# Zeros for the output: two transfers from SyncE's queue, or twelve from ScalarE's

## The chip, the cores and the metric

One Trainium2 chip; the kernel runs on one of its cores. The metric is device microseconds of the whole program, lower is better. Engines: TensorE (PE, with its weight loads as PEld), VectorE (DVE), ScalarE (ACT), GpSimd (POOL) and SyncE (SP). SP and ACT issue plain DMAs, POOL the indirect ones (gathers and scatters by a list of rows).

## The reference

A linear attention whose output feeds a mixture of 8 experts, of which each of 3072 tokens uses two:

```python
# attention: q, k, v [4, 8, 768, 64], in blocks of 64 with a decaying state
intra = (qb @ kb.T * Dmask) @ vb
inter = (qb * lam_pow) @ kv_state
x = attn_out.transpose(0, 2, 1, 3).reshape(3072, 512)
# mixture
noisy = x @ w_gate + log1p(exp(x @ w_noise)) * noise      # [3072, 8]
top2 = argpartition(-noisy, 2)[:, :2]; w = softmax of the two
out = zeros((3072, 512))
for e in range(8):
    for k in range(2):
        mask = top2[:, k] == e
        h = maximum(x[mask] @ w1[e], 0)                   # w1[e] 512 x 1024
        out[mask] += w[mask, k] * (h @ w2[e])             # w2[e] 1024 x 512
```

Everything is float32. A token that is not expert 0's gets its first contribution by an addition into `out`, so `out` has to hold zeros before the experts write to it.

## The kernel before, in words

The program has three stretches.

**Attention** goes in 12 steps (`for t in range(NST)`), two chunks of 128 tokens each. Each step stores its rows to a DRAM tensor `x_tok` (`store_x`, L443) and computes gate logits.

**Routing** is done in three groups of chunks, 0 to 7, 8 to 15 and 16 to 23. For each chunk and each of its two choices POOL scatters 128 records (token number and weight, 8 bytes each) to the lists `lst` in DRAM: 48 scatters (`scatter_list`, L634), handed out one to three at a time by `paced`, which first copies one element of a tile that the scatter is to come after (`spacer`, L682). The lists of the other experts are read back with `load_rec` (L880, L882): `recz` for expert 0, `rec` for the rest. The first `rec` load needs all 48 scatters; the second `recz` load needs those of the first two groups, 32 scatters. They stand on SP's queue, which is worked through in order.

**Experts**: expert 0 is computed in three parts of 2, 2 and 3 tiles of 128 tokens (`PARTS0`, the last tile 64). In each part eight blocks of the first layer (`mm1`, 12 matmuls each, L1037, into one of four PSUM banks `pS`) are evacuated by ACT (`ht`, L1043) and DVE (L1047), then `gemm2` (24 matmuls a tile, L1078, or 16 for the last) follows. In the third part, between the `gemm2` of its tiles, PE transposes the rows that POOL has gathered for expert 1 (`trans_rows`, L898, from `gather_rows`, L889). PE works in program order, so it stands there until the gather has landed. The weights of expert 1 (`w1`, six loads, L770) are loaded from SP's queue after the second part. The experts' outputs are scattered into `out` from expert 1's first layer on (`scatter_out`, L1135).

The zeros for `out` come from one 128 x 512 tile `zero`, read again and again: 24 blocks of 128 rows, 6 MB in all. The tile is later also the output tile of expert 0's last `gemm2` (`PV`, L1089).

The order is that of the program. For DMAs of SP and ACT together the framework hands out eight semaphores in turn (DMAHW0 to DMAHW7), in the order in which it expects the DMAs to be issued; a DMA is issued when the one that had its semaphore before has landed. POOL's DMAs have eight others (DMASW0 to DMASW7).

Of the kernel before, what the change touches and what calls it, by code (L numbers as in the profile page):

```python
# [35 lines left out]
DM = H * D  # L36
# [4 lines left out]
NTOK = B * S  # L41
# [25 lines left out]
LOADS = {2: [(1, 0)], 3: [(1, 1)], 4: [(1, 2)], 5: [(1, 3)], 9: [(2, 0), (2, 1)], 10: [(2, 2)], 11: [(2, 3)]}  # L67
HIGH = {4: [(1, 0)], 5: [(1, 1)], 6: [(1, 2)], 7: [(1, 3)], 10: [(2, 0), (2, 1)]}
LOW = {5: [(1, 0)], 6: [(1, 1)], 7: [(1, 2)], 10: [(2, 0)]}
ZEROS = {11: 8}  # L70
LATE = (6, 7)
MID = 16
X1 = ((), (), (), (), (0, 1), (2, 3, 4), (5, 6))
# [17 lines left out]
def size(e, t):  # L91
    return TS if t < NT - 1 else TAILS[e]
# [31 lines left out]
def kernel(  # L124
# [3 lines left out]
    nc = tc.nc  # L128
# [22 lines left out]
    def load(u, nm):  # L151

        if u >= NST:
            return
        b, w = divmod(u, NW)
        at = b * H * S * D + w * 2 * C * D
        store, src, n = {"qt": (QT, q, 2), "kt": (KT, k, 2), "vt": (VT, v, 3)}[nm]
        store[u] = aw.tile([128, 2, H, D], FT, name=nm, bufs=n)
        for a in range(2):
            nc.sync.dma_start(store[u][:, a], sub(src, at + a * C * D, [[D, 128], [S * D, H], [1, D]]))  # L160
# [36 lines left out]
    p = psum.tile([128, H], FT, name="pL")  # L197
# [13 lines left out]
    p = psum.tile([128, HP, C], FT, name="pL")  # L211
# [88 lines left out]
    def scatter(n):  # L300
        for job in scatters[:n]:
            scatter_list(*job)
        del scatters[:n]
# [11 lines left out]
    def trans_k(u):  # L315

        kT[u] = aw.tile([128, HP, 2, C], FT, name="kT", bufs=1)
        for a in range(2):
            p = bank()
            for hp in range(HP):  # L320
                nc.tensor.transpose(p[:, hp, :], KT[u][:, a, 2 * hp:2 * hp + 2, :], identf)
            if u:
                nc.scalar.activation(kT[u][:, :, a, :], p, AF.Copy)
            else:
                nc.vector.tensor_copy(kT[u][:, :, a, :], p)
# [62 lines left out]
    def intra(u):  # L388
        for hp in range(HP):
            for a in range(2):  # L390
                for s in range(2):
                    add_out(u, a, hp, s, VT[u][:, a, 2 * hp + s, :], AT[u][hp // 2][:, s, hp % 2, a, :])
# [28 lines left out]
    def products(u):  # L421

        p = psum.tile([128, 2, C], FT, name="pR")
        for d in range(DB):
            nc.tensor.matmul(p[d * 32:(d + 1) * 32], wgn[:, d, :], XO[u][:, :, d, :], start=True, stop=True)
        XP[u] = aw.tile([128, 2, C], FT, name="xp", bufs=1)
        nc.scalar.activation(XP[u], p, AF.Copy)
# [3 lines left out]
    def turn_x(u):  # L431

        XC[u] = aw.tile([128, 2, DB, C], FT, name="xc")
        for a in range(2):
            p = bank()
            for d in range(DB):
                nc.tensor.transpose(p[:, d, :], XO[u][:, a, d, :], identf)  # L437
            nc.scalar.activation(XC[u][:, a], p, AF.Copy)

    def store_x(u):  # L440

        queue = nc.gpsimd if u < NST - 4 else nc.sync
        queue.dma_start(x_tok[2 * u * C:2 * (u + 1) * C, :].rearrange("(a p) m -> p a m", a=2),  # L443
                          XC[u].rearrange("p a d i -> p a (d i)"))
# [235 lines left out]
    def paced(n, tile):  # L680
        if scatters:
            nc.gpsimd.tensor_copy(spacer, tile[0:1, 0:1])  # L682
            scatter(n)
# [9 lines left out]
    for n in range(2):  # L693
        o, m = n * DB * CAP, DB * TX * TS
# [149 lines left out]
    def split_low(which, e, j, half=None, low=nc.vector):  # L844
        for st, hi, lo in split_parts(which, e, j, half):
            low.tensor_tensor(lo, st, hi.bitcast(FT), op=SUB)
# [182 lines left out]
    def columns(e, t0, n):  # L1029
        return slice(t0 * TS, min((t0 + n) * TS, FULL + TAILS[e]))  # L1030
# [19 lines left out]
    def ht(e, part, f, c):  # L1050

        at = c.start + (0 if not part else TAILS[e] if c.start >= FULL else CAP + TAIL)
        return HT[0].rearrange("p (f c) -> p f c", f=FB)[:, f, at:at + c.stop - c.start]
# [90 lines left out]
    zero = consts.tile([128, DM], FT, name="zero")  # L1144
# [4 lines left out]
    def zero_out(n):  # L1149
        i = list(itertools.islice(zeros, n))  # L1150
        if i:
            nc.sync.dma_start(out[i[0] * 128:(i[-1] + 1) * 128, :].rearrange("(a p) m -> p a m", p=128),
                              zero[:, None, :].to_broadcast([128, len(i), DM]))

    for t in range(NST):
        u = t + 1
        if t:
            products(t - 1)
            turn_x(t - 1)
            if t == 8:  # L1160
                split_low(1, 0, 3, low=nc.gpsimd)
        if u < NST:
            trans_k(u)
        load(t + 3, "kt")
        if u < NST:
            trans_q(u)
        load(t + 3, "qt")
        if u < NST:
            kv(u)
        if t:  # L1170
            store_x(t - 1)
            paced(1, XC[t - 1][:, 1, 0, :])
        if t not in LATE:
            kdecay(t + 2)
        if u == NST:
            scatter(1)
        if u == NST:
            logits(t - 1)
        intra(t)
        load(t + 3, "vt")  # L1180
        inter(t, 0)
        evac_o(t)
        if t in LATE:
            kdecay(t + 2)
        paced(1, XO[t][:, 1, 0, :])
        if t and u < NST:
            logits(t - 1)
        if 2 * t in GB[1:]:
            if 2 * t > GB[1]:
                finish(GB.index(2 * t) - 2, False)  # L1190
            jobs.append(routing(GB.index(2 * t) - 1))
        advance(FILLB)
        if u < NST:
            scores(u)
            inter(u, 1)
        for which, j in HIGH.get(t, []):
            split_high(which, 0, j)
        if u < NST:
            if LOW.get(t):
                nc.gpsimd.tensor_copy(spacer, AT[u][0][0:1, 0, 0, 0, 0:1])  # L1200
            for which, j in LOW.get(t, []):
                split_low(which, 0, j, low=nc.gpsimd)
            paced(1, AT[u][1][:, 1, 0, 0, :])
        advance(FILLA.get(t, 18))
        for which, j in LOADS.get(t, []):
            load_w(which, 0, j)
        zero_out(ZEROS.get(t, 0))
        if t == 2:
            turn_noise()
        if t == 4:  # L1210
            for i in range(4):
                nc.sync.dma_start(sub(lst, i * 128 * LI * RW, [[LI * RW, 128], [1, LI * RW]]), linit)
# [30 lines left out]
    for i, (t0, n) in enumerate(parts(0)):  # L1243
        for f in range(FB):
            if i or f >= 2:
                gemm1(0, t0, n, f)
            if i == 0:
                if 1 <= f < 5:
                    split_w(2, 0, 2 + (f > 2), (f - 1) % 2)
                if f == 2:  # L1250
                    nc.scalar.activation(XG[6], zero, AF.Copy)
                advance(FILL1)
            if i == 1 and f < 4:
                advance(FILL2)
                if f == 3:
                    finish(2, False)
            if i or f >= 2:
                paced(1 + (i == 2), ht(0, 0, f, columns(0, t0, n)).bitcast(FT))
            if i == 1 and f == 2:
                load_rec(0, 1)  # L1260
            if i == 2 and f == 2:
                load_rec(1, 0)
                load_rec(0, 2)
                load_rec(0, 3)
                for j in range(1, 3):
                    load_rec(1, j)
                for t in range(NT):
                    gather_rows(1, t)
            if i == 2 and f >= 4:
                for j in X1[f - 4]:  # L1270
                    trans_rows(j, size(1, j))
        if i == 0:
            zero_out(NTOK // 128)
            advance(50)
        if i == 1:
            which_expert(1, nc.sync)
            which_list(1, nc.sync)
            for j in range(4):
                load_w(1, 1, j)
        for t in range(t0, t0 + n):  # L1280
            if i < 2:
                paced(3, PV[t - 1] if t > t0 else ht(0, 0, FB - 1, columns(0, t0, n)).bitcast(FT))
            for _ in gemm2(0, t):
                pass
            if t == 0:
                advance(50)
            for j in {0: (2, 3), 2: (4, 5, 6)}.get(t, ()):
                trans_rows(j, size(0, j))
            if i == 2:
                for j in range((0, 2, 4)[t - t0], (2, 4, 4)[t - t0]):  # L1290
                    split_w(1, 1, j)
                    load_w(2, 1, j)
                for j in X1[t]:
                    trans_rows(j, size(1, j))
# [225 lines left out]
    with tc.For_i(0, n_over) as it:  # L1520
# [16 lines left out]
        for f in range(FB):  # L1537
            p = psum.tile([128, OV], FT, name="pS", bufs=4)
# [7 lines left out]
        p = psum.tile([OV, DM], FT, name="pO")  # L1546
# [35 lines left out]
```

## Time and profile before

| | us |
|---|---|
| median of 3 runs | 692.43 (691.93 to 693.0) |
| the profiled execution | 693.23 |
| its span, from the first to the last instruction | 691.4 |
| PE busy in the span | 671.6 (97%) |
| granted TensorE clock, mean | 0.994 |

How to read it: times in the rows below are microseconds from the span's start. The first two columns of a row of the timeline are its start and its length; what stands in square brackets is how long the engine sat idle before it and what ended that. An SPq or ACTq row is the issue of a DMA by that engine's sequencer; the transfer itself comes after it. "To landing" is from the issue to the arrival of the DMA's semaphore. In the tables of windows the columns give each engine's busy time, and at the end the granted clock, the busy share of the 16 DMA engines and the rate.

### The profile page before, as it was taken

Reading aid. Unit: us, or ns where it says so; the run is one execution under the profiler, and the core shown is the slowest. Engines: PE = TensorE matmul, PEld = TensorE weight load, DVE = VectorE, ACT = ScalarE, POOL = GpSimd, SP = SyncE. Lnnn points to the kernel's source line nnn. Section 1 sums busy time; section 2 is a strip of 40 time slices with the busy share of each in tenths; the row PEclk is TensorE's granted clock in tenths of the full one; section 3 lists DMA queues with packets and bytes.
Section 4 is the critical chain, followed back from the end, with each engine's and each line's share of the span. In section 5 each row is a group of like instructions: output and inputs, shape, how many; then the busy total and the mean of one; then the engine's idle time right before and its main releaser. Section 6 shows DMA issues by size and latency. Waiting matters only on the chain.

```text
span 691.4 us, 13961 instructions
## 1 busy us (share of the span) xinstructions
PE 671.6 (97%) x4861; PEld 598.1 (87%) x4861; DVE 482.4 (70%) x1060; ACT 309.5 (45%) x634; POOL 370.0 (54%) x474
## 2 busy tenths in 40 slices
PE   7899999899999999999999999999999999999995
PEld 4788888698898898899989998998898899889984
DVE  6335888878436566789867886889596979588610
ACT  2667786441133332365437434653363356327400
POOL 7111355678854555776358536753773667264332
PEclk9999999999999999999999999999999999999998
DMA  9999999576517437766477547854875576464033
GB/s 205 214 233 262 229 252 250 163 245 163 113 32 221 136 119 171 175 177 191 149 183 188 189 149 178 221 175 142 166 235 158 126 195 189 122 135 116 1 46 40
DMA packets 151901, 115.06 MB, mean 166 GB/s; under 512 B 88063, under 2 KB 123007, under 8 KB 151828
## 3 DMA queue, kind: packets, MB, share of 16 engines
q1 hardware_dynamic: 137636, 84.04, 44.8%
q0 software_dynamic: 13776, 29.57, 20.5%
q8 instruction: 39, 0.64, 0.4%
q10 hardware_dynamic: 416, 0.53, 0.3%
q14 instruction: 34, 0.28, 0.1%
HBM read 77.58 MB, written 37.32 MB: 166 GB/s over the span
## 4 chain that ended last, share of the span: by engine, by line
PE 68%; DVE 12%; issue 8%; POOL 4%; DMA 3%; SPq 2%; ACT 1%; POOLq 1%; DVEq 0%
PE pS L993 15%; PE pKV L1078 13%; PE pO L1078 10%; PE pS L1037 7%; PE pS L1110 5%; PE pS L364 3%; PE pKV L377 2%; POOL lst L634 2%; PE pO L377 2%; SPq L160 2%; PE pR L993 1%; POOL out_dram L1135 1%; DMA xr<-x_tok,rec 1%; DVE ht L1004 1%; PE pS L437 1%
## 5 line engine op out<-in xcount | busy, mean ns | idle before, releaser
L993 PE MATMUL pS<-xa,w 128*128 128x400 f32 (+1 forms) x624 | 158.0, 343 | 0.3 <-ACT gt L1012 0.2
L818 POOL TENSOR_TENSOR wst<-wst 128x256 f32<-128x256 f32 x96 | 96.4, 1016 | 84.1 <-DVE w L810 81.7
L993 PEld LDWEIGHTS pS<-xa,w 128*128 128x128 f32 x624 | 113.2, 188 | 4.6 <-DVE w L810 2.0
L1135 POOL DMA_INDIRECT out_dram<-ot,rec x40 | 73.6, 1839 | 75.5 <-DVE ot L1094 56.2
L1078 PE MATMUL pKV<-w2h,ht 128*128 128x512 f32 x336 | 109.0, 394 | 0.0
L1078 PE MATMUL pO<-w2h,ht 128*128 128x512 f32 x336 | 108.4, 392 | 0.0
L993 PE MATMUL pS<-xb,w 128*128 128x400 f32 (+1 forms) x240 | 81.6, 340 | 0.0
L1078 PEld LDWEIGHTS pKV<-w2h,ht 128*128 128x128 f32 x336 | 63.2, 188 | 14.3 <-DVE gt L1094 0.6
L1078 PEld LDWEIGHTS pO<-w2h,ht 128*128 128x128 f32 x336 | 63.1, 188 | 13.5
L1037 PE MATMUL pS<-xa,w 128*128 128x256 f32 (+2 forms) x440 | 73.5, 316 | 0.8 <-DVE xa L901 0.4
L1037 PEld LDWEIGHTS pS<-xa,w 128*128 128x128 f32 x440 | 65.3, 189 | 4.9 <-DVE xa L901 0.6
L1078 PE MATMUL pKV<-w2l,ht 128*128 128x512 f32 x168 | 65.8, 391 | 0.0
L1078 PE MATMUL pO<-w2l,ht 128*128 128x512 f32 x168 | 65.7, 391 | 0.0
L961 ACT ACTIVATE xa<-wst 128x512 fp32r<-128x512 f32 (+1 forms) x48 | 25.1, 568 | 79.5 <-DVE wst L970 72.3
L810 DVE TENSOR_TENSOR w<-wst,w 128x512 fp32r<-128x512 f32 (+2 forms) x72 | 59.6, 844 | 0.1
L889 POOL DMA_INDIRECT xr<-x_tok,rec x42 | 46.2, 1101 | 19.2 <-issue 6.5
L634 POOL DMA_INDIRECT lst<-recs,dest x48 | 49.7, 1035 | 10.8 <-issue 8.5
L1012 ACT ACTIVATE ot<-pS 128x400 f32<-128x400 f32 (+1 forms) x60 | 29.7, 495 | 48.8 <-PE pS L993 44.6
L808 ACT ACTIVATE w<-wst 128x512 fp32r<-128x512 f32 (+2 forms) x72 | 48.1, 692 | 5.3 <-POOL wst L818 5.2
L1004 DVE SCALAR_TENSOR_TENSOR ht<-ot,ht 128x400 fp32r<-128x400 f32 (+1 forms) x60 | 45.4, 756 | 1.5 <-ACT ht L1001 0.8
L993 PEld LDWEIGHTS pS<-xb,w 128*128 128x128 f32 x240 | 45.0, 188 | 0.6 <-DVE xb L962 0.3
L1043 ACT ACTIVATE ht<-pS 128x256 fp32r<-128x256 f32 (+2 forms) x40 | 17.9, 448 | 59.5 <-PE pS L1037 58.2
(287 smaller groups left out, 1367.0 us busy)
## 6 DMA issues: line engine op xcount, KB each, us to landing
wst<-in_moe_w_dram SPq DMA_DIRECT2D x36, 512.0 KB, 5.4
wst<-in_moe_w_dram SPq DMA_DIRECT2D x32, 256.0 KB, 3.3
kt<-in_k_dram SPq DMA_DIRECT2D x24, 256.0 KB, 5.6
qt<-in_q_dram SPq DMA_DIRECT2D x24, 256.0 KB, 6.7
vt<-in_v_dram SPq DMA_DIRECT2D x24, 256.0 KB, 5.3
wst<-in_moe_w_dram SPq DMA_DIRECT2D x48, 128.0 KB, 3.4
wst<-turned SPq DMA_DIRECT2D x96, 64.0 KB, 2.0
turned<-w1b SPq DMA_DIRECT2D x20, 256.0 KB, 2.8
```

What stands on the lines that cost most here:

```text
L634: st = nc.gpsimd.indirect_dma_start(out=lst, out_offset=bass.IndirectOffsetOnAxis(ap=r["dest"][:, i, c:c + 1], axis=0), in_=r["rec"][:, c, ...
L808: nc.scalar.activation(hi[:, ks], src, AF.Copy)
L810: nc.vector.tensor_tensor(lo[:, ks], src, hi[:, ks].bitcast(FT), op=SUB)
L818: g.tensor_tensor(o, x, y, op=op)
L889: nc.gpsimd.indirect_dma_start(out=xrow(e, t)[:size(e, t)], out_offset=None, in_=x_tok[:rows, :], in_offset=bass.IndirectOffsetOnAxis(ap=a ...
L993: nc.tensor.matmul(p, WO[f % 2][:, a, kw, d, :], xo(x, kx, kx + 1)[:, 0, d, :w], start=first and i == 0, stop=i == 5, skip_group_check=True)
L1004: return lambda: nc.vector.scalar_tensor_tensor(hv(e, 1, i, k), src, 0.0, hv(e, 0, i, k).bitcast(FT), op0=OP.max, op1=SUB)
L1012: nc.scalar.activation(banks[m], U, AF.Copy)
L1037: nc.tensor.matmul(p, W1[a][d][:, fs], xt(b, cs)[:, d], start=(d == 0 and i == 0), stop=(d == DB - 1 and i == 2))
L1078: nc.tensor.matmul(p, h, W2[b][f // 2][:, f % 2, :], start=(i == 0), stop=(i == len(TERMS) - 1))
L1110: nc.tensor.matmul(p, W2[b][f // 2][:, f % 2, d * 128:(d + 1) * 128], h, start=(i == 0), stop=(i == len(TERMS) - 1))
L1135: st = nc.gpsimd.indirect_dma_start(out=out, out_offset=bass.IndirectOffsetOnAxis(ap=REC[e, t][:, 0:1], axis=0), in_=o, in_offset=None, bo ...
```

## The change

The two calls that wrote 8 and 16 blocks from SP are gone (the first was in attention step 11, the second between the first layer and the `gemm2` of expert 0's first part). In the second and third part, `zero_out(2)` stands behind each block of the first layer, and issues from ACT's queue. The iterator holds 24 blocks, so twelve calls issue something, two blocks (512 KB) each: eight in the second part and four in the third.

```diff
-ZEROS = {11: 8}
...
     def zero_out(n):
         i = list(itertools.islice(zeros, n))
         if i:
-            nc.sync.dma_start(out[i[0] * 128:(i[-1] + 1) * 128, :].rearrange("(a p) m -> p a m", p=128),
-                              zero[:, None, :].to_broadcast([128, len(i), DM]))
+            nc.scalar.dma_start(out[i[0] * 128:(i[-1] + 1) * 128, :].rearrange("(a p) m -> p a m", p=128),
+                                zero[:, None, :].to_broadcast([128, len(i), DM]))
...
             load_w(which, 0, j)
-        zero_out(ZEROS.get(t, 0))
         if t == 2:
...
             if i or f >= 2:
                 paced(1 + (i == 2), ht(0, 0, f, columns(0, t0, n)).bitcast(FT))
+            if i:
+                zero_out(2)
             if i == 1 and f == 2:
                 load_rec(0, 1)
...
         if i == 0:
-            zero_out(NTOK // 128)
             advance(50)
```

ACT before, from the transposes ahead of the second part to the first split of expert 1's weights (`ht` 128x256: second part, 128x320: third part):

```order
L900 ACTIVATE xa<-pS 128x4x128 [waits PE_49] x2
L1043 ACTIVATE ht<-pS 128x256 [waits PE_49] x8
L900 ACTIVATE xa<-pS 128x4x128 [waits PE_49] x2
L900 ACTIVATE xa<-pS 128x4x64 [waits PE_49]
L1043 ACTIVATE ht<-pS 128x320 [waits PE_49] x8
L842 ACTIVATE w_314<-wst_161 128x1024 [waits DMAHW2_49]
```

ACT now, from the end of the second part on, in the third part:

```order
L899 ACTIVATE xa<-pS 128x4x128 [waits PE_49] x2
L899 ACTIVATE xa<-pS 128x4x64 [waits PE_49]
L1042 ACTIVATE ht<-pS 128x320 [waits PE_49]
L1151 DMA out_dram<-zero 128x2x512 [waits DMAHW6_49]
L1042 ACTIVATE ht<-pS 128x320 [waits PE_49]
L1151 DMA out_dram<-zero 128x2x512 [waits DMAHW7_49]
L1042 ACTIVATE ht<-pS 128x320 [waits PE_49]
L1151 DMA out_dram<-zero 128x2x512 [waits DMAHW0_49]
L1042 ACTIVATE ht<-pS 128x320 [waits PE_49]
L1151 DMA out_dram<-zero 128x2x512 [waits DMAHW1_49]
L1042 ACTIVATE ht<-pS 128x320 [waits PE_49] x4
L841 ACTIVATE w_314<-wst_161 128x1024 [waits DMAHW5_49]
```

A zero transfer stands behind each of the first four evacuations, and behind each of the eight in the second part; the brackets name the semaphores that ACT waits for before it issues one.

SP before, from the first zeros to the first load of expert 1's `w1` (`recz` and `rec` are reads of the lists):

```order
L1152 DMA out_dram<-zero 128x8x512 [waits DMAHW5_49]
L443 DMA x_tok<-xc 128x2x512 [waits DMAHW6_49,Activation_49]
L882 DMA recz_2394<-lst 128x4 [waits DMASW1_49]
L1152 DMA out_dram<-zero 128x16x512 [waits DMAHW0_49]
L882 DMA recz_2846<-lst 128x4 [waits DMAHW1_49,DMASW6_49]
L758 TENSOR_LOAD order [waits DVE_49]
L758 ISA x2
L762 TENSOR_LOAD order [waits DVE_49]
L762 ISA x2
L770 ISA
L770 DMA wst_161<-in_moe_w_dram 128x1024 [waits DMAHW2_49,DVE_49,PE_49]
```

SP now, from the first read of a list to the second half of the second `w1` tile:

```order
L881 DMA recz_2393<-lst 128x4 [waits DMAHW6_49,DMASW1_49]
L881 DMA recz_2847<-lst 128x4 [waits DMAHW3_49,DMASW6_49]
L757 TENSOR_LOAD order [waits DVE_49]
L757 ISA x2
L761 TENSOR_LOAD order [waits DVE_49]
L761 ISA x2
L769 ISA
L769 DMA wst_161<-in_moe_w_dram 128x1024 [waits DMAHW5_49,DVE_49,PE_49]
L769 ISA
L769 DMA wst_162<-in_moe_w_dram 64x1024 [waits DMAHW7_49,DMAHW2_49,DVE_49]
L769 ISA
L769 DMA wst_162<-in_moe_w_dram 64x1024 [waits DMAHW1_49]
```

The two zero transfers have left SP's queue and nothing else in it has changed its place. The two halves of the second `w1` tile now have the semaphores DMAHW7 and DMAHW1, the ones that the second and the fourth zero transfer of the third part wait for.

## Rows read from the trace of the kernel before

**Rows 1.** The page's busy time, share of span and instructions by engine

```profile
PE 671.6 (97%) x4861; PEld 598.1 (87%) x4861; DVE 482.4 (70%) x1060; ACT 309.5 (45%) x634; POOL 370.0 (54%) x474
```

**Rows 2.** Windows: busy time by engine (instructions), clock, DMA share, rate

```profile
core 0: us, PE busy (x) PEld busy (x) DVE busy (x) ACT busy (x) POOL busy (x), PEclk, DMA share, GB/s
...
160.00:211.00 51.00, 51.00 (x335) 46.44 (x332) 22.38 (x78) 10.91 (x23) 37.46 (x70) 1.00 0.41 90
211.00:640.00 429.00, 428.15 (x2231) 386.84 (x2231) 335.48 (x599) 198.94 (x386) 244.31 (x255) 1.00 0.63 168
```

**Rows 3.** Chain of waits, 196 to 216 us: start, length, what

```profile
199.81 4.08 DMA lst<-recs,dest
...
203.90 1.61 DMA rec<-lst
...
206.29 0.36 POOL xr L889
...
207.65 3.47 DMA xr<-x_tok,rec
...
211.16 0.66 PE pS L898 x4
```

**Rows 4.** Timeline of TensorE's weight loads at 211 us

```profile
211.16 0.42 PEld L898 LDWEIGHTS pS<-identf,xr 128*128 128x128 f32 x4 [0.31 <-DMA xr<-x_tok,rec]
```

**Rows 5.** Timeline of SP's DMA issues, 132 to 186 us

```profile
132.83 0.88 SPq L1152 DMA_DIRECT2D out_dram<-zero  x1
...
148.78 0.52 SPq L1152 DMA_DIRECT2D out_dram<-zero  x1
179.21 0.35 SPq L882 DMA_DIRECT2D recz<-lst  x1
181.28 4.41 SPq L770 DMA_DIRECT2D wst<-in_moe_w_dram  x6
```

**Rows 6.** Windows of the large zeros, of the weight loads, and after them

```profile
151.00:164.00 13.00, 12.74 (x85) 10.86 (x84) 12.35 (x59) 1.86 (x4) 11.24 (x23) 1.00 1.05 328
...
182.00:193.00 11.00, 11.00 (x61) 9.34 (x60) 3.12 (x5) 1.50 (x4) 9.25 (x21) 1.00 0.99 190
194.00:204.00 10.00, 10.00 (x70) 10.00 (x70) 2.89 (x11) 2.62 (x6) 5.70 (x13) 1.00 0.02 2
```

**Rows 7.** Tile lst: the 9 list scatters of 149 to 163 us

```profile
DMA to landing us min/median/max: 6.4/8.6/9.2
```

**Rows 8.** Tile lst: the 9 list scatters of 164 to 181 us

```profile
DMA to landing us min/median/max: 2.1/2.7/3.8
```

**Rows 9.** Tile lst: the 6 list scatters of 181.5 to 190 us

```profile
DMA to landing us min/median/max: 7.4/8.3/8.6
```

**Rows 10.** Tile lst: the 3 list scatters of 190.1 to 193.5 us

```profile
DMA to landing us min/median/max: 4.8/5.9/7.1
```

**Rows 11.** Tile x_tok: the 512 KB store of 143.1 us

```profile
DMA to landing us min/median/max: 4.2/4.2/4.2
```

**Rows 12.** Timeline of ScalarE: evacuations of the second and third part

```profile
171.44 0.38 ACT L1043 ACTIVATE ht<-pS 128x256 fp32r<-128x256 f32 x1 [1.06 <-PE pS L1037]
...
198.14 0.44 ACT L1043 ACTIVATE ht<-pS 128x320 fp32r<-128x320 f32 x1 [1.32 <-PE pS L1037]
```

**Rows 13.** Timeline of ScalarE: the longer of its two DMA issues

```profile
4.99 0.40 ACTq L200 DMA_DIRECT2D powd<-pwt  x1
```

**Rows 14.** DMA issues of 181 to 186 us: count, KB each, median to landing

```profile
wst<-in_moe_w_dram SPq DMA_DIRECT2D x4, 256.0 KB, 9.4
```

**Rows 15.** Tile x_tok: the 3 gathers of 169.2 to 172.0 us

```profile
DMA to landing us min/median/max: 3.4/4.6/4.8
```

**Rows 16.** Timeline of TensorE: the transposes of those gathered rows

```profile
183.94 1.43 PE L898 MATMUL pS<-identf,xb 128*128 128x128 f32 x12
```

**Rows 17.** Timeline of ScalarE and VectorE at 143 us

```profile
142.97 0.39 ACT L1043 ACTIVATE ht<-pS 128x256 fp32r<-128x256 f32 x1
...
143.39 0.42 DVE L1047 SCALAR_TENSOR_TENSOR ht<-pS,ht 128x256 fp32r<-128x256 f32 x1 [2.38 <-DMA out_dram<-zero]
```

## The prediction, made before the changed kernel ran

> **What bounds the kernel now.** I read the page's busy times first. TensorE is busy 671.6 of 691.4 us [rows 1], so a change elsewhere counts only where it makes TensorE stand or lets it stand less. The windows say where that can be: from 160 to 211 us it is busy without a gap, and from 211 to 640 us for 428.15 of 429 us [rows 2]. What delays it at 211 us therefore arrives at the end undiminished; what helps something else in between is worth nothing.
>
> The chain of waits shows why 211 us is the place to look at. There the chain is not TensorE's. It comes from POOL, which scatters list records one after another; the last scatter is issued at 199.81 and lands 4.08 us later, at 203.89, then SP reads the list (1.61), POOL issues gathers, and TensorE's transposes start at 211.16, when the second gather has landed [rows 3]. In TensorE's own row the weight load of these transposes has waited 0.31 us for that gather [rows 4]. So two paths end together at 211 us: TensorE's own work, and scatter, list, gather. There is no spare time on the second; a later last scatter costs its whole delay, an earlier one gains at most 0.31 us.
>
> SP's issues and the windows tell what the zeros do today. They are issued at 132.83 (2 MB) and 148.78 (4 MB) [rows 5]; the second keeps the 16 DMA engines full from 151 to 164 us, at 328 GB/s [rows 6]. From 194 to 204 us, where the last scatters are on their way, these engines are 0.02 busy [rows 6].
>
> **The change, part by part.** *Issuing.* Twelve issues on ACT at 0.40 us, the longer of the two that ACT has in the trace [rows 13], are 4.8 us. Each stands behind an evacuation that is followed by 1.06 us of idle time in the second part and 1.32 us in the third [rows 12], so all of it is hidden and costs nothing; were that cover gone, the evacuation behind would be late, and TensorE has four PSUM banks before it notices. SP loses 0.88 and 0.52 us of issues [rows 5] on a queue that then waits for scatters until 179.21: worth nothing. The tile `zero` is written again behind expert 0's last `gemm2`, and `out` is first scattered into during expert 1; both stand behind the transposes at 211 us, and the last piece is there before (below).
>
> *When the pieces travel.* In the second part evacuations follow each other every 0.38 + 1.06 = 1.44 us [rows 12]. A 512 KB piece at 328 GB/s [rows 6] takes 1.60 us. So eight pieces, issued from 168 to 179 us, make a continuous bulk of 12.8 us, about 169 to 183 us. In the third part the spacing is 0.44 + 1.32 = 1.76 us [rows 12]; the four pieces go out behind evacuations that end at 193.3, 195.1, 196.8 and 198.6. One such transfer by itself lands 4.2 us after its issue, by a store of the same size [rows 11], so the last lands at 202.8 at the earliest.
>
> *What bulk does to scatters.* This is the term that counts, and the trace of before has it three times over. Scatters issued while the large zeros ran landed after 6.4 to 9.2 us, in the middle 8.6 [rows 7]; without bulk after 2.7 [rows 8]; under the weight loads after 8.3 [rows 9]; those issued in the last three microseconds of these loads (182 to 193 us [rows 6]) after 5.9, at most 7.1 [rows 10].
>
> [...]
>
> *First consequence: weight loads start later.* SP's second list read waits for the 32nd scatter. SP went on at 179.21 [rows 5], and with 2.7 us to landing [rows 8] that scatter was issued at about 176.5. In the second part's bulk it lands after 8.6 us [rows 7], at 185.1, which is 5.9 us later. The `w1` loads then start at 187.2 in place of 181.28 [rows 5], and their 11 us of full DMA engines [rows 6] run to about 199 instead of 193, with the third part's zeros among them. They themselves are not missed: even the slow ones, 9.4 us to landing [rows 14], are there by some 201 us, and the first split that needs them stands behind the third part's eighth evacuation, four spacings of 1.76 after the fourth, at 205.6. Their lateness matters only because they now overlap the last scatters.
>
> *Second consequence: the last scatter.* It is issued at 199.81 by a POOL that works through its scatters without regard to the zeros. From below: with no bulk left it lands as before, 0, or −0.31 if the chain shortens a little. From above: in full bulk it lands after 8.3 us [rows 9], at 208.1, which is +4.2. I take the rows that it is nearest to: it is issued some 3 us before the last piece lands, like the scatters of [rows 10], which took between 5.9 in the middle and 7.1 at most; the mean of the two is 6.5. Landing: 206.3, +2.4 us. List read and gathers behind it are free of bulk and keep their durations.
>
> *The second part's gathers.* Three gathers issued until 172.0 landed in 3.4 to 4.8 us [rows 15] and are needed at 183.94 [rows 16]. Under bulk I give them 8.6 + (4.6 − 2.7) = 10.5 us, so the last is there at 182.5 with 1.4 us to spare. From above, if the three hold each other up by 1.9 us each, it is 172.0 + 8.6 + 5.7 = 186.3 and TensorE stands 2.4 us; I take 0.
>
> *Sum*, against the profiled execution (693.23 us, 1.8 more than its span, and 0.8 over the median of the runs): 0 + 0 + 2.4 + 0 = +2.4, so 695.6 there and 694.8 us against the median of 692.43.
>
> **The rivals.** *The last scatter is out of reach (not slower).* If the second part's pieces, 1.60 us each against a spacing of 1.44, leave gaps, the 32nd scatter lands nearly as before and the weight loads are over by 195. The third part's pieces leave gaps too (1.60 of 1.76), and the last scatter meets one piece, not a queue. For it: the single 512 KB store lands in 4.2 us [rows 11]. Against it: three stretches of bulk, all with over 5 us more [rows 7, 9, 10]. It decides whether the last scatter lands before 205.3, that is with less than 1.4 us of delay. Time 692.4 to 693.8.
>
> *ACT is held up (worse).* The second piece of the third part waits for the semaphore of the first half of the second weight tile. That half was issued about 0.6 us after 181.28; with 9.4 us [rows 14] and the 5.9 us above it lands at 197.2, and the piece is due at 195.1. ACT, and the evacuations queued behind the piece, then stand 2.1 us. Four banks cover TensorE, but the pieces slip, bulk lasts until 204 or later, and the last scatter gets the full 8.3 us: +4.2, and up to 2 more if POOL's pacing copies come late with the evacuations. Time 696.6 to 698.6.
>
> *The early stretch gains (faster).* DVE's row at 143.39 names the zeros as what ended 2.38 us of idle time [rows 17]. Were that so, and if the scatters later came to no harm, 2.4 us could be won: 690.0. Against it: ACT's evacuation, whose result that instruction reads, ends at 142.97 + 0.39 = 143.36 in the same rows, so without the zeros DVE would have stood there all the same.
>
> That the change doesn't do what it says can be left out: twelve issues stand in ACT's order, none in SP's.
>
> **How the numbers follow.** Forecast 0.47, out of reach 0.30, ACT held up 0.15, early gain 0.08. The forecast's own range is 693.2 to 696.6, by the bounds of the scatter's term. The range over the cases leaves out most of the early gain and the far end of the held-up case: 692.1 to 697.8. About 0.2%, 1.4 us, is what a measurement here can tell from no change. Slower: 0.42 of the forecast's 0.47 (the rest has under 1.4 us) and 0.15 make 0.57, and a little of the second case 0.58. Faster 0.07, within 0.2% 0.35.
>
> **What would show it.** Right: DMA engines full from 169 to 183; SP's second list read at 184 to 186 in place of 179.21, and the weight loads 5 to 6 us later; the last scatter issued near 199.8 and landed 6 to 7 us later; TensorE standing some 2.5 us before the transposes at 211, with all later work moved by as much. Wrong: the list read at 179 to 181, or the last scatter landed by 205. Held up: an ACT row of the third part that waits for a weight load. Wrong in another way: a gap of TensorE at 184, before the transposes of the gathered rows.

## The result, and the profile after

The changed kernel takes 701.64 us (median of 5 runs, 701.41 to 702.5), the kernel before beside it 692.45 (691.93 to 694.59): 1.0112 times, 95% interval 1.0089 to 1.0136. Forecast were 694.8 us: the sign was right, a loss of 9.2 us where 2.4 were expected. On two other chips the same pair gave 1.0124 and 1.0139. The profiled execution took 701.41 us, 8.2 more than that of before, and its span grew by as much, 691.4 to 699.6.

The page's busy times, as in [rows 1]:

```profile
PE 675.0 (96%) x4861; PEld 600.9 (86%) x4861; DVE 482.1 (69%) x1060; ACT 309.2 (44%) x634; POOL 371.3 (53%) x474
```

The instructions are the same in number. PE is busy 3.4 us longer, and stands 4.8 us longer (8.2 less 3.4). Laying the two traces' PE instructions side by side by their order shows where. The first matmuls of expert 0's third part, before and then after:

```profile
190.91 1.76 PE L1037 MATMUL pS<-xa,w 128*128 128x320 f32 x11
```

```profile
190.01 0.30 PE L1036 MATMUL pS<-xa,w 128*128 128x320 f32 x1
191.05 1.73 PE L1036 MATMUL pS<-xa,w 128*128 128x320 f32 x10 [0.74 <-DVE xa L900]
```

After comes to that part 0.9 us ahead, which is no gain of the change (the kernel before, run again as b_again below, comes to it at 190.00 too), stands 0.74 us behind its first matmul, and from the second matmul on the two are within 0.1 us of each other. At the end after is 8.1 us behind. So all of the loss comes after 191 us. The chain of waits there, to be read against [rows 3]:

```profile
200.17 7.90 DMA lst<-recs,dest
...
208.08 1.55 DMA rec<-lst
...
211.77 5.48 DMA xr<-x_tok,rec
...
217.30 1.11 PE pS L897 x4
218.41 6.54 PE pKV L1077 x24
```

The last scatter lands after 7.90 us, not 4.08; the list read keeps its length; the gather takes 5.48 us, not 3.47; PE's transposes start at 217.30, not 211.16. The timeline of PE shows the two gaps in brackets, and something else in the lengths:

```profile
213.92 1.11 PE L897 MATMUL pS<-identf,xr 128*128 128x128 f32 x4 [3.15 <-DMA xr<-x_tok,rec]
217.30 1.11 PE L897 MATMUL pS<-identf,xr 128*128 128x128 f32 x4 [2.27 <-DMA xr<-x_tok,rec]
218.06 0.78 PE L1077 MATMUL pKV<-w2h,ht 128*128 128x512 f32 x1
...
224.56 0.39 PE L1077 MATMUL pKV<-w2h,ht 128*128 128x512 f32 x1
```

Four transposes take 1.11 us (0.66 in [rows 3]) and the first matmul behind them 0.78, the last 0.39. The windows say why: the granted clock, 1.00 throughout in [rows 2], falls at the gap.

```profile
core 0: us, PE busy (x) PEld busy (x) DVE busy (x) ACT busy (x) POOL busy (x), PEclk, DMA share, GB/s
...
200.00:205.00 5.00, 5.00 (x36) 5.00 (x36) 1.67 (x6) 1.31 (x3) 0.99 (x2) 1.00 1.03 263
205.00:210.00 5.00, 5.00 (x24) 4.12 (x23) 0.56 (x2) 2.33 (x3) 0.00 (x0) 1.00 0.09 12
210.00:215.00 5.00, 1.85 (x8) 1.00 (x6) 3.02 (x3) 0.00 (x0) 3.89 (x3) 0.87 0.40 101
215.00:220.00 5.00, 2.73 (x10) 2.32 (x10) 1.38 (x2) 2.15 (x4) 3.87 (x4) 0.50 0.97 340
220.00:225.00 5.00, 5.00 (x23) 4.06 (x22) 0.01 (x1) 0.94 (x1) 0.57 (x3) 0.95 0.30 109
```

From 215 to 220 us it is 0.50, after PE was busy only 1.85 of the 5 us before. The first row bears on the scatter: from 200 to 205 the DMA engines are full, where [rows 6] has 0.02 for 194 to 204. SP's issues show what else has moved:

```profile
185.06 0.34 SPq L881 DMA_DIRECT2D recz<-lst  x1
187.15 5.42 SPq L769 DMA_DIRECT2D wst<-in_moe_w_dram  x6
208.08 0.34 SPq L879 DMA_DIRECT2D rec<-lst  x1
...
212.71 1.51 SPq L772 DMA_DIRECT2D wst<-in_moe_w_dram  x2
```

The second list read and expert 1's `w1` loads are 5.9 us later than in [rows 5]. The loads of `w2` go out at 212.71, when the second gather (211.77) is under way. In the trace of before that gather has landed by 211.12, and they go out behind it:

```profile
212.60 8.18 SPq L773 DMA_DIRECT2D wst<-in_moe_w_dram  x4
```

So the 8.1 us are, by rows: the last scatter's landing, 203.89 to 208.07, 4.2; from there to the second transposes 9.2 us instead of 7.3, 2.0 (the gather's 5.48 less 3.47); the slower PE behind them 1.5, that is 1.11 less 0.66 for the transposes and 6.54 for the 24 matmuls less the 5.51 that they take in before (211.82 to 217.33 us, where the clock is 1.00) and in `e6_warm`, below. The last 0.5 us are spread over the rest of the program.

### The profile page after: what moved, and what is told of

It is laid out like the page before. It is cut to its first block, busy times and chain, and to the rows that moved or that the text cites. A ratio compares the mean times of both kernels' runs of the same rounds, so it can differ in the third digit from the quotient of the medians.

```text
span 699.6 us, 13977 instructions
## 1 busy us (share of the span) xinstructions
PE 675.0 (96%) x4861; PEld 600.9 (86%) x4861; DVE 482.1 (69%) x1060; ACT 309.2 (44%) x634; POOL 371.3 (53%) x474
## 4 chain that ended last, share of the span: by engine, by line
PE 66%; DVE 10%; issue 8%; DMA 5%; POOL 5%; SPq 4%; ACT 1%; POOLq 1%; DVEq 0%; ACTq 0%
PE pS L992 16%; PE pKV L1077 11%; PE pO L1077 9%; PE pS L1036 6%; PE pS L1109 5%; PE pS L363 2%; PE pKV L376 2%; POOL lst L633 2%; PE pO L376 2%; SPq L159 2%; DMA xr<-x_tok,rec 2%; SPq L934 1%; PE pR L992 1%; POOL out_dram L1134 1%; PE pS L436 1%
```

## The experiments

Three questions: which pieces do it, whether the second gather and the clock are terms of their own, and how a piece holds up a scatter. Every row of the table is one profile and one timing beside the kernel before on the same chip. "Pieces" are those issued in the first, second and third part of expert 0. The lag runs from the last scatter's issue to its landing, which is where SP's list read starts. PE's wait is that of its transposes for the first two gathers of expert 1's rows (in e1 and e9 PE also stands 0.9 and 1.0 us for the third).

| kernel | pieces | lag, us | PE's wait, us | time to before |
|---|---|---|---|---|
| before | SP's two transfers | 4.1 | 0 | |
| b_again (before once more) | same | 4.4 | 1.8 | 0.9997 [0.9980, 1.0015] |
| e5_no_zeros | none | 4.2 | 2.9 | 1.0003 [0.9988, 1.0017] |
| e3_first_part | 12, 0, 0 | 4.1 | 0 | 0.9999 [0.9970, 1.0027] |
| e1_second_part | 0, 8, 0 | 4.2 | 1.4 | 1.0009 [0.9986, 1.0032] |
| e1b_second_again | 0, 8, 0 | 5.1 | 0.9 | 1.0005 [0.9980, 1.0030] |
| e7_first_second | 4, 8, 0 | 4.4 | 0 | 1.0031 [0.9997, 1.0065] |
| e9_two_third | 2, 8, 2 | 5.3 | 0.8 | 1.0016 [0.9997, 1.0036] |
| e2_third_part | 0, 0, 4 | 6.4 | 2.5 | 1.0023 [1.0001, 1.0045] |
| e2b_third_again | 0, 0, 4 | 6.4 | 6.3 | 1.0068 [1.0030, 1.0105] |
| e10_later_third | 0, 8, 4 later | 6.3 | 2.6 | 1.0061 [1.0033, 1.0089] |
| after | 0, 8, 4 | 7.9 | 5.4 | 1.0112 [1.0089, 1.0136] |
| a_again | 0, 8, 4 | 10.9 | 8.6 | 1.0124 [1.0101, 1.0147] |
| a_third | 0, 8, 4 | 8.7 | 7.1 | 1.0139 [1.0115, 1.0163] |

The kernel before itself ran at 692.5 and 693.4 us on two of the chips, at 697.3 on a third and at about 700.5 on two more (e1 to e5; e1b, e2b, e7, e8); in the profiles of these two PE is 1.3 to 4.6 us late already at the first matmul of the second part (166.00 us in the first trace of before), ahead of the last scatter and all that follows it. So ratios are compared and not times.

On these two chips ScalarE's evacuations of the third part also come in fits, in every profile, with zeros or without. In before the first one starts 1.95 us after the part's first matmul (192.86 and 190.91), in e2b and in e5, which writes no zeros, 5.0 us. POOL's pacing copies come after the evacuations (one stood 1.9 us for ScalarE in each of these two), so the last scatter is issued late by amounts that differ from profile to profile. What holds ScalarE up there is not shown. So of these eight runs the lags can be compared; their waits and times hold that lateness too, and the changed kernel itself was not timed on these chips.

### Which pieces

```diff
-            if i:            # after: second and third part
+            if i == 1:       # e1: second part alone, eight blocks left with SP
+            if i == 2:       # e2: third part alone, sixteen blocks left with SP
+            if i == 0:       # e3: all in the first part
+                             # e5: the call is gone, no zeros are written
                 zero_out(2)
```

> Eight blocks go out from SP in attention step 11 as before, the other sixteen as eight pieces from ACT in the second part; none in the third. Theory A (the second part's bulk makes the list read and with it the weight loads 6 us late, and only these late loads together with the third part's pieces hold the last scatter up): list read at about 185, weight loads to about 198, last scatter landed by 205.5, TensorE standing at most 1.5 us at 211; 693 to 695.5 us. Rival B (the third part's pieces alone hold the last scatter up): within 1 us of the kernel before, 692 to 693.5, since there are none. Rival C (ScalarE's queue as such makes scatters slow): last scatter as late as in the changed kernel, 699 or more.

> Sixteen blocks go out from SP where they did before (eight in attention step 11, eight behind the first part's first layer), the last eight as four pieces from ACT in the third part. Theory A: the list read stays at 179, the weight loads at 181 to 193, the pieces meet no queue; last scatter landed by 205.5, 692.4 to 694.5 us. Rival B: last scatter landed at 207 or later, TensorE standing 3 us or more, 698 to 701 us. Rival C: as B.

> All twelve 512 KB pieces from ACT's queue, but in the first part (one behind each block of its first layer, two ahead of each of its two second-layer tiles), so that they are over by about 167 us. Theories A and B (place alone counts): as the kernel before, 692 to 693.5 us, list read at 179 to 180, last scatter landed at 204. Rival C (the queue or the cutting counts): 695 us or more.

> Left out: the zeros are not written at all. What the zeros cost in the kernel before, at most the 0.3 us that TensorE waited at 211: 691.8 to 692.8 us by theories A and B alike. If the early stretch gained by their leaving, as one rival of the prediction had it: 690 us or less.

The times alone decided little: all four within 0.25% of before. The lags did: 4.1 to 4.2 us in the three without pieces in the third part, 6.4 in the one with them. e2's wait of 2.5 us stays short of the 3 us that rival B asked for. e5 answers a second question: with no zeros at all, nothing is won. PE waits 2.9 us in it with a lag of 4.2, because there the scatter is issued at 206.38, and PE is ready for the transposes 7.9 us after that; in before it is ready 10.7 us after the scatter's issue. The wait depends on that distance as well as on the lag.

> The eight pieces of the second part alone (the other eight 128-row blocks go out in one transfer of SP's, where the first of the kernel before stood), once more on another chip. Theory, the loss comes from the third part's pieces: the last scatter lands 4 to 4.5 us after its issue, and what is left is DVE's wait for the late list and a thinner margin, 1.000 to 1.003 of the kernel before. Rival, the second part's pieces push w1's loads so late that these are the cause: the last scatter lags 6 us or more and the ratio is 1.006 or above.

> The four pieces of the third part alone (the other sixteen blocks go out in two transfers of SP's, at the places of the kernel before), once more. Theory: the last scatter, issued while they are under way, lands 6 to 8 us after its issue and PE waits for the second expert's rows; 1.004 to 1.009 of the kernel before, since w1's loads are 3 us earlier than in the changed kernel and do not share the engines with the pieces. Rival, pieces and w1 only hurt together: the lag is 4 to 4.5 us and the ratio within 1.002 of 1.

> All twelve pieces from ACT, four in the first part and eight in the second, none in the third. Theory: as the second part alone, last scatter 4 to 4.5 us after its issue, second gather 3.4 to 3.7 us, 1.000 to 1.003 of the kernel before. Rival, that it is ACT's queue or the cutting into pieces itself: 1.008 or above, as in the changed kernel.

e1b and e7 lie within their uncertainty of 1, e2b at 1.0068, with an interval that overlaps e7's. e1b's lag of 5.1 us is above the expected 4 to 4.5. e7 has all twelve pieces on ACT's queue and eight of them where the change put them; TensorE's transposes in it wait for nothing that a gather ends (a weight load of theirs stood 0.4 us for one, as 0.31 in [rows 4]):

```profile
213.71 0.60 PE L897 MATMUL pS<-identf,xr 128*128 128x128 f32 x4
214.49 0.66 PE L897 MATMUL pS<-identf,xr 128*128 128x128 f32 x4 [0.18 <-issue]
```

So neither ACT's queue nor the cutting makes the lag (4.4 us in e7); the pieces of the third part do (6.4 in e2 and e2b). The times that show it best stand on one chip: a_third, the changed kernel once more, at 1.0139, and e9 (below), in which only two of the four pieces of the third part have moved to the first part, at 1.0016. From their chains of waits, a_third's last scatter and then e9's:

```profile
200.32 8.68 DMA lst<-recs,dest
```

```profile
199.23 5.25 DMA lst<-recs,dest
```

The chain of e2b, which has the third part's pieces alone, shows the same two steps as after:

```profile
204.18 6.36 DMA lst<-recs,dest
210.55 1.62 DMA rec<-lst
214.30 5.16 DMA xr<-x_tok,rec
219.50 1.11 PE pS L898 x4
```

Not all of e2b's wait comes from these steps: PE is ready for the transposes 7.9 us after the scatter's issue there, 10.6 in after. Its lag is 1.5 to 4.5 us shorter than in the three traces of after, where the late `w1` loads travel beside the pieces; in e2b they are issued from 183.4 us and their full stretch is over by 194. That the second part's pieces add to the loss in this way fits the lags, and is not shown by a run that changes the loads alone.

### Is the loss of one chip, and is the edge older than the change

> The changed kernel as it is, once more, so that the three others of this set stand beside it on one chip. If its loss lies in the stretch where the second expert's rows arrive (last scatter under the zeros, second gather beside the loads of w2), its time is again 1.008 to 1.013 of the kernel before, and its trace shows the last scatter landing 7 to 8 us after its issue, PE idle for 4 to 6 us behind the two gathers of 210 to 217 us, and the granted clock down to about 0.5 in one window of 5 us after that. If the loss was of one chip alone, the ratio is within 1.002 of 1.

> The kernel before as it is, for a second trace of it on the same chip as the changed one. If what the first trace of it shows is the rule, its last scatter lands 4 us after its issue, PE does not wait more than 0.5 us for the gathers of the second expert's rows, and the clock stays at 1.00 from 160 us on. If PE waits there for 2 us or more here as well, the stretch was on the edge before the change, and a chip decides how much of the change's loss is seen.

The loss is the rule, at 1.0124 here and at 1.0139 on a third chip. Its size in this trace is above what was expected: a lag of 10.9 us for 7 to 8, and 8.6 us of PE's wait for 4 to 6. The chain of a_again, with the longest lag of all:

```profile
201.08 10.87 DMA lst<-recs,dest
...
215.64 5.30 DMA xr<-x_tok,rec
```

b_again shows that the kernel before stands on the edge that [rows 4] showed with 0.31 us. Its PE timeline:

```profile
210.82 0.66 PE L898 MATMUL pS<-identf,xr 128*128 128x128 f32 x4 [1.08 <-DMA xr<-x_tok,rec]
212.24 0.91 PE L898 MATMUL pS<-identf,xr 128*128 128x128 f32 x4 [0.76 <-DMA xr<-x_tok,rec]
```

Here PE waits 1.8 us without any change, and the granted clock goes to 0.75 from 210 to 215 and 0.91 from 215 to 220; expected were at most 0.5 us and a steady clock, or else 2 us and more.

### The second gather and the clock

```diff
+ hold = dram.tile([1, 4], FT, name="hold")
+ # e4: SP's w2 loads stand behind a small DMA that reads the transposed second tile
+ if t == t0:
+     nc.sync.dma_start(hold, xt(0, slice(TS, 2 * TS))[0:1, 0, 0:4].bitcast(FT))
  for j in js:
      load_w(2, 1, j)
+ # e6: matmuls of no use ahead of each of the two groups of transposes
+ p = psum.tile([128, 384], FT, name="pR")
+ for _ in range((20, 14)[j]):
+     nc.tensor.matmul(p, ones, ones[:, None, :].to_broadcast([128, 3, 128]), start=True, stop=True)
```

> The changed kernel with SP's loads of the second expert's w2 held back until the second gather has reached its tile. Theory (the second gather took 5.48 us instead of 3.47 because those loads, issued at 212.7 and 213.9 us, ran beside it): the second gather takes 3.5 to 4 us again and PE goes on 1.2 to 2 us earlier, so 699.5 to 700.5 us where the changed kernel has 701.6. Rival (the second gather was long because POOL issued it later and slower, 1.83 instead of 1.04 us): its time stays at 5 to 5.5 us and the kernel is the same within 0.5 us, or slower if the w2 loads then come late for their first matmul.

> The changed kernel with 20 and 14 matmuls of no use put ahead of the first transposes of the two gathers, so that PE is busy while it waits for them. Theory (the granted clock falls to 0.50 at 215 to 220 us because PE stands idle before it, and that costs 1.2 us on top of the wait): the clock stays at 1.00 from 205 to 230 us and the kernel gains 1 to 1.5 us on the changed one. Rival (the matmuls behind the gathers wait for the rows or for DVE's copies in any case): the clock stays up and the time does not move by more than 0.3 us, or loses up to 1 us where the added matmuls end after the rows have come.

e4: 701.52 us against a_again's 704.46, 1.0079 [1.0059, 1.0098]. Its loads go out at 220.11, and the second gather is short again:

```profile
214.08 3.66 DMA xr<-x_tok,rec
```

That is 3.66 us against 5.30, 1.6 us by the trace; the rest of the 2.9 us that were timed is the shorter lag of this profile (9.1 us), or variation. POOL's own time for that gather, the rival, stays at 1.32 us (1.31 in a_again) and explains nothing. Across the profiles the gather is long (5.2 to 5.5 us) where the `w2` loads are issued 0.3 to 0.9 us behind it (after, a_third, e2b), and short (3.4 to 3.7) where they come 2.4 us behind it or later (before, b_again, e4, e10).

e6: 702.42 us, 1.0086 [1.0061, 1.0110]. Its chain from the first transposes on:

```profile
217.55 1.07 PE pS L897 x4
218.63 3.54 PE pR L1296 x14
222.16 0.44 PE pS L897 x4
222.60 5.51 PE pKV L1077 x24
```

The 24 matmuls take 5.51 us, against 7.81 in a_again and 6.54 in after. So the clock is a term of its own, 1.0 to 2.3 us in them. The added matmuls did not hold it at 1.00 all the time, as expected (0.77 from 215 to 220 and 0.89 from 220 to 225; PE still stood 2.32 us after the first twenty), and the fourteen stood in PE's way for 3.5 us, part of it wait that there was anyway. The net, 2.0 us, is above the expected 1 to 1.5; the lag of this profile is 1.3 us shorter too, and the interval overlaps a_again's [1.0101, 1.0147] a little.

> The changed kernel with both earlier edits, the held loads of w2 and the matmuls of no use, which alone brought 1.0079 and 1.0086 where the changed kernel stood at 1.0124 on the same chip. If collision and clock are separate terms, the gains add: 1.003 to 1.005, and what is left is the late last scatter and DVE's wait for the list. If they are one (a shorter wait already keeps the clock up), it stays at 1.007 to 1.008.

Both edits together gave 1.0087 [1.0054, 1.0119], not the 1.003 to 1.005 of gains that add. That decides nothing: e8 ran on one of the two chips with the late evacuations, without the changed kernel, e4 or e6 beside it. In its trace `pKV` took 5.50 us and PE waited for no gather, but its last scatter was issued at 206.34, five us later than in a_again, and the added matmuls kept PE until 221.3. Whether the two terms add stays open.

### How a piece holds up a scatter

```diff
-            if i:
+            if i == 1 or (i == 0 and f >= 6) or (i == 2 and f < 2):   # e9
+            if i == 1 or (i == 2 and f >= 4):                         # e10
                 zero_out(2)
```

> The changed kernel as it is, beside the two others on one chip: 1.008 to 1.013 of the kernel before, last scatter 7.5 to 11 us from issue to landing.

> Two pieces in the third part instead of four, the other two moved to the end of the first part. If bytes queued ahead decide, the two pieces of 1 MB, issued 193 to 195 us, are written by 200 us, the last scatter lands 4 to 4.5 us after its issue, and the time is 1.000 to 1.003 of the kernel before. If any piece in the third part costs, the lag is 5.5 us or more and the ratio 1.004 to 1.007.

> The third part's four pieces issued four steps later, about 200 to 205.5 us, so that at most one stands ahead of the last scatter of 200 to 201 us. If bytes queued ahead decide, the scatter lands after 4 to 5 us, but the pieces are still being written until 210 to 213 us, beside the list's read and the first gather: these take 1 to 3 us more than 1.6 and 3.3 us, 1.003 to 1.008 of the kernel before. If any piece under way beside the scatter costs, its lag is again 6.5 us or more, and the ratio 1.008 or above.

a_third came out at 1.0139, just above what was expected, with a lag of 8.7 us.

e10 was to tell what is queued ahead of a scatter from what travels beside it. ACT's issues of the pieces and POOL's last scatter, from the two timelines:

```profile
198.99 0.38 ACTq L1151 DMA_DIRECT2D out_dram<-zero  x1
200.75 0.63 ACTq L1151 DMA_DIRECT2D out_dram<-zero  x1
```

```profile
198.91 0.98 POOL L633 DMA_INDIRECT lst<-recs,dest  x1 [0.16 <-issue]
```

By the starts of the rows not one piece is issued before the scatter, three within 3.6 us after it (the third at 202.51), the fourth only at 207.16, when it has landed. Still it takes 6.3 us to land. But POOL's instruction lasts 0.98 us, until 199.89, and the first piece is issued within it. The DMA engines are idle until the first piece fills them:

```profile
198.75:199.75 1.00, 1.00 (x9) 1.00 (x8) 0.30 (x1) 0.44 (x1) 0.84 (x2) 1.00 0.02 1
199.75:201.25 1.50, 1.50 (x12) 1.50 (x11) 0.30 (x3) 0.44 (x1) 0.14 (x1) 1.00 0.90 324
```

And the DMA view by queues (packets, MB, share of the 16 engines) has ACT's queue, q10, at work first, from 199.2 to 201.3 us, and the batch of POOL's queue, q0, behind it, from 201.3 to 201.7 (a few packets of each stand in the other stretch):

```profile
q10 hardware_dynamic: 244, 0.49, 64.8%
```

```profile
q0 software_dynamic: 30, 0.00, 6.2%
```

In before the like batch begins 1.57 us after the last scatter's issue, here 2.45. So by these packets the first piece was ahead of the scatter in the engines, and the next two went beside the rest of its way. Both theories stay: of the 2.2 us that the lag is longer than in before, 0.9 are gone by the time that batch moves and 1.3 come after it. Neither expectation was met whole, the lag of 6.3 us being above 4 to 5 and just under 6.5, the ratio of 1.0061 that of the first; and the gather, which by the first should have taken 1 to 3 us more, took 3.71. e9 lies between its two expectations in the lag (5.3 us) and within the first in the ratio (1.0016): its two pieces and the `w1` loads fill the engines until 200 us (1.02 from 195 on, 0.09 from 200 to 205), and the scatter of 199.23 comes at their end.

## Why the prediction was right in direction and wrong in size

*Issuing: right.* ACT's four issues of the third part take 0.38 us and follow the evacuations at 1.76 us, none held up (the timeline has them at 192.98, 194.74, 196.50 and 198.26). That refutes the rival of the held-up ACT, although its time (696.6 to 698.6) lay nearer.

*List read and weight loads: right.* Predicted 185.1 and 187.2, measured 185.06 and 187.15, and by the mechanism named: the scatter that the read waits for, issued at 176.88, took 8.2 us to land (2.7 in before). One effect was overlooked: VectorE scales `gemm2`'s result with what that list read brings, and stood for it.

```profile
188.72 0.75 DVE L1093 TENSOR_SCALAR xb<-pO,recz 128x512 f32<-128x512 f32 x1 [10.14 <-DMA recz<-lst]
```

TensorE stood 0.74 us for it at 191. It costs nothing here, since PE stands 20 us later for the gathers in any case.

*The second part's gathers: right in the outcome, not in the price.* There is no wait before their transposes at 183.04. But under the bulk they landed after 4.8 to 5.5 us, where the prediction gave them 10.5; in before it was 3.4 to 4.8 [rows 15]. What bulk adds to a scatter was not what it added to these gathers, and the margin of 1.4 us was larger than thought.

*The last scatter: the step that failed first.* The prediction took 6.5 us, as for a scatter in the last three microseconds of a bulk that ends at 202.8. But it had itself put the late `w1` loads among the pieces, and the engines are full until 205 (1.03 from 200 on). The scatters issued from 192.5 to 201 us, in the view of their tile:

```profile
DMA to landing us min/median/max: 7.9/8.0/8.1
```

That is the upper bound of the prediction's term, +4.2, and not the 2.4 that it took; a_again's 10.87 lies beyond the bound. Against the 4.1 us of before, the extra delay is 3.8 us in after and 6.8 in a_again.

*"List read and gathers behind it are free of bulk and keep their durations": failed.* The bulk of the zeros is over by then. But SP's `w2` loads wait for VectorE's split of `w1`, which comes after its scaling of the third part's first `gemm2`; PE let that scaling start at 210.80 in after and at 210.69 in before, while the second gather was issued 4.1 us later. The chain slipped into the loads: 2.0 us, priced at nothing. (In a_again the scaling itself stood for a list read, until 214.15 by an estimate from VectorE's 0.85 us of busy time between 210 and 215; the gather, from 215.64 on, took 5.30 us all the same.)

*The clock: a term that was missing.* The prediction let PE stand and then go on at its old speed; the lower clock, 0.50 from 215 to 220 us, cost 1.5 us.

*"A later last scatter costs its whole delay": right*, and more than right. 4.2 us of delay became 8.1.

*Rivals.* "Out of reach" fell with the landing at 208.07. "The early stretch gains" fell with e3 and e5: with the zeros moved or gone, no measurable gain. No version tried beats the kernel before. The lower end of the forecast's own range, 693.2, does not follow from the bounds of the scatter's term, as it says: with a term of 0 it would be 692.4. Nothing else rests on it.

## What to carry to other kernels

Where two paths end together, as [rows 4] showed, price a delay at least whole, and then look at what the late chain slips into: which transfers go out at another engine's pace (here SP's `w2` loads), and what PE's clock does after its wait (0.50 in after, behind 5.4 us). Keep small indirect writes that feed a chain from sharing the DMA engines with large transfers, even ones that another queue issues in the same microsecond (e10's scatter took 6.3 us, before's 4.1). Before bulk is moved for a gain, leave it out once: if its absence gains nothing (e5, 1.0003), a better place for it will hardly gain more. And look for what else differs between two profiles before a wait is put down to the edit: here ScalarE's lateness on two chips (5.0 us behind the third part's first matmul in e5, 1.95 in before) moved the last scatter as well (206.38 and 199.81 us).

## What the runs showed of the hardware

PE stood 5.4 us in after between 210 and 218 us, and the granted clock was 0.50 from 215 to 220; it stood 1.8 us in b_again, and the clock was 0.75 from 210 to 215; in e9 it stood 0.8 us, and the clock stayed at 1.00 from 205 to 225. The length of the wait alone does not decide it: in e5 PE stood 2.9 us and in e10 2.6 us, and the clock was 1.00 in every window from 205 to 225, as in this row of e10 from 210 to 215:

```profile
210.00:215.00 5.00, 2.64 (x15) 2.14 (x16) 4.14 (x5) 1.89 (x3) 4.09 (x4) 1.00 0.68 229
```

A matmul of 128x512 took 0.63 to 0.78 us in after from 218 to 220 us (granted clock 0.50), and 0.39 from 205 to 210 (1.00). A scatter of 128 records, whose instruction on POOL began 0.08 us before the first of three 512 KB writes of another queue was issued, landed after 6.3 us (e10) instead of 4.1 to 4.4 (before, b_again). Three gathers of rows, issued under the eight such writes of the second part in after, landed after 4.8 to 5.5 us instead of 3.4 to 4.8 (before).
